# Moving the store of the pairs' decay rows ahead of the second and third weight tiles, in a planned attention-and-two-MLP kernel

## The chip, the cores and the metric

The kernel runs on one core of one Trainium2 chip. The metric is the device time of one execution in microseconds (us), as the median of several runs. A core has TensorE (PE in the profile), VectorE (DVE), ScalarE (ACT), GpSimd (POOL) and SyncE (SP). Nearly every DMA of this kernel is issued from SP's instruction queue and served by 16 DMA engines.

## The reference

Causal attention with a decay per position, then two MLPs with a squared ReLU:

```python
scores = scale * np.matmul(q, k.transpose(0, 1, 3, 2))       # q, k, v: (4, 8, 576, 64)
cum = np.cumsum(np.log(np.clip(f, 0.0001, 1.0)), axis=-1)    # f: (4, 8, 576)
decay = cum[:, :, :, None] - cum[:, :, None, :]
scores = np.where(causal, -1000000000.0, scores + decay)
attn = softmax(scores)
x = (attn @ v) as (2304, 512)
x = np.maximum(x @ moe_w_in, 0.0) ** 2 @ moe_w_out           # 512 -> 2048 -> 512
return np.maximum(x @ moe2_w_in, 0.0) ** 2 @ moe2_w_out
```

## The kernel before

Nothing is written in program order by hand. Each piece of work is an `op(engine, duration, function, priority, dependencies, buffers)`. The planner `Plan.run` (line 106) plays all of them through with the given durations and picks, whenever an engine is free, the ready op with the lowest priority number; the order in which it picks is the order in which the instructions are emitted. Ops that may run on either of two engines (`either`, line 324) get the one that is free in that play. So a change in one op's priority or dependencies can reorder every engine from there on.

The work has these stages.

- **Head.** SP loads `f`, the first 64 positions of q and k (`load_qk`, L469) and the first weight tile in two halves (L798). DVE and ACT make the log and the running sum of `f` (L1335 to L1349). L472 stores the first 64 positions' decay rows beside q and k. `first_part` (line 458) does the attention of the first 64 positions, for two halves of the heads: scores L486, softmax L492 to L502, transposes L514, product with v L526, and the split of the result into a high and a low part (L541, L543), which is the input of the first MLP block.
- **Pairs.** `pair` (line 555) does positions 64 to 191, for two heads at a time, 16 times. q and k come by L567, the decay rows by L570 from the buffer `aug2_d` in DRAM, v by L573. The scores are L589, the maximum L409 on DVE, the exponential L417, the normalisation L605 (ACT) or L607 (DVE or POOL), the transposes L615, their copy L618, the product L628/L629, the copy to X L636.
- **Weights.** Meanwhile the 16 tiles of the first MLP (`weights`, line 783) are loaded in an integer form (L798, 1024 KB each) into three staging buffers (`st`, `ph`, `tmp`), decoded on DVE by L816, L818 and L820 (the last tile by L823 to L829), and split into a high part on ACT (L833) and a low part on DVE (L837).
- **First MLP and the remaining attention.** Blocks of 12 matmuls (L861 into `hp`, L936 into `yp`) fill PE between the attention's pieces; between the two, `hidden` squares the ReLU (L870, then L873 on DVE, L880 on ACT or L877 on POOL) and splits it (L883, L886). `unit` (line 643) does positions 192 to 575 of each head (L713, L731, L750).
- **Second MLP.** L1233 and L1259, from about 600 us to the end.

PE also has filler matmuls (L1384) that the planner puts where PE would stand idle in the head.

The op that is changed is `store2` (line 1362, the DMA is L1363): one DMA of 96 KB from X to `aug2_d`, which all 16 pairs read through L570. Its values are written by `times8_act` (L1360, on ACT). Before the change it depends on those and on `first_loads` (the four L472 stores), with priority -1.0e7. The second half of the first weight tile has priority U + 3 and the v loads of the head U + 4 and U + 5, where U is -1.0e9; a lower number goes first.

Of the kernel before, what the change touches and what calls it, by code (L numbers as in the profile page):

```python
# [69 lines left out]
class Plan:  # L70
# [17 lines left out]
    def op(self, eng, dur, fn, prio, deps=(), uses=(), data=None, other=None, dmas=1, rows=128):  # L88


        o = Op()
        o.how, o.uses, o.data, o.dmas, o.rows, o.turn = {eng: (dur, fn, 0)}, tuple(uses), data, dmas, rows, dur == self.TURN[0]
        if other:
            o.how[other[0]] = (other[1], other[2], 1)
        o.prio = (prio, len(self.ops))
        o.outs, o.ready, o.nwait = [], 0.0, 0
        for d in deps:
            if d is not None:
                d.outs.append(o)
                o.nwait += 1  # L100
        for b in o.uses:
            b.left += 1
        self.ops.append(o)
        return o
# [122 lines left out]
def act(n, psum=False):  # L227
    return (0.052 if psum else 0.093) + 0.00083 * n
# [34 lines left out]
def attention_then_two_squared_relu_mlps(  # L263
# [26 lines left out]
    P = Plan()  # L290
    op = P.op
# [69 lines left out]
    U = -1.0e9  # L361
# [921 lines left out]
    with tc.manual_schedule():  # L1283
# [81 lines left out]
        def parts(y):  # L1365
            if y == 0:
                nc.scalar.mul(out=ch, in_=f_cum, mul=8.0)
            elif y == 1:
                nc.vector.scalar_tensor_tensor(out=cl, in0=f_cum, scalar=8.0, in1=f32(ch), op0=ALU.mult, op1=ALU.subtract)
            else:  # L1370
                nc.scalar.mul(out=nh, in_=f32(ch), mul=-1.0)
                nc.scalar.mul(out=nl, in_=f32(cl), mul=-1.0)
# [25 lines left out]
        first_done, first_loads = [], []  # L1398
# [1 line left out]
            first_part(y, -1.0e8 + y)  # L1400
        o = op("DVE", 0.67, scan1, -1.0e7, [o_f])
        o_8 = op("ACT", 2 * act(QA), times8_act, -1.0e7, [o, o_m1])
        aug_second = [op("SP", P.COPY[0], store2, -1.0e7, [o_8] + first_loads, data=0.3)]
        o_p = op("ACT", act(S), lambda: parts(0), TUNE["PP"], [o] + first_done)
        o_p = op("DVE", dvs(S), lambda: parts(1), TUNE["PP"], [o_p])
        o_p = op("ACT", 2 * act(S), lambda: parts(2), TUNE["PP"], [o_p])
# [118 lines left out]
```

## Time and profile before

| what | before |
|---|---|
| median of 3 runs | 972.8 us (972.77 to 976.41) |
| profiled execution, own time | 977.94 us |
| its span, first to last instruction | 976.2 us |
| PE busy | 948.3 us (97%) |
| DVE / ACT / POOL busy | 683.6 / 453.1 / 361.4 us |
| mean granted PE clock | 0.982 of full speed |

Full speed of the clock is 2.4 GHz, and 0.50 is the lower level, 1.2 GHz. Busy times are sums over an engine's instructions; "idle before" is the time for which an engine stood still just ahead of an instruction, with what released it. Where a stretch lists "PE 62.0 of 68.0", the rest is idle.

### The profile page before, as it was taken

How to read it: one execution, taken by the hardware profiler on the slowest of the kernel's cores; microseconds unless marked ns; L12 is line 12 of the kernel's file. 1: busy time of each engine (PE TensorE's matmuls, PEld its weight loads, DVE VectorE, ACT ScalarE, POOL GpSimd, SP SyncE). 2: the span in 40 equal slices, each digit the busy share in tenths (PEclk: the TensorE clock that was granted, in tenths of full speed). 3: DMA queues.
4: the chain of work that ended last, by engine and by line, in shares of the span. 5: the costliest groups of instructions: out<-in, count | busy, mean ns of one | idle time of the engine just before them, and what ended most of it. 6: DMA issues, size and time to landing. Idle time of an engine off the chain costs nothing.

```text
span 976.2 us, 17134 instructions
## 1 busy us (share of the span) xinstructions
PE 948.3 (97%) x6463; PEld 866.7 (89%) x6463; DVE 683.6 (70%) x1341; ACT 453.1 (46%) x900; POOL 361.4 (37%) x315
## 2 busy tenths in 40 slices
PE   6999999999999999999999999999999999999997
PEld 3888898999997999999999998988898988989886
DVE  7998667787768778876478689888874445734343
ACT  3686677777777678775333353223230112311011
POOL 2244443444434435434232435332351314522130
PEclk7799999999999999999999999999999999999999
DMA  8767245666656756755546524674452111322113
GB/s 251 253 202 207 83 104 119 140 129 146 132 110 134 148 122 134 143 118 120 120 160 207 173 82 157 199 242 159 134 171 88 64 65 65 117 86 79 65 65 108
DMA packets 177187, 131.91 MB, mean 135 GB/s; under 512 B 140944, under 2 KB 155536, under 8 KB 175056
## 3 DMA queue, kind: packets, MB, share of 16 engines
q1 hardware_dynamic: 176848, 130.32, 49.1%
q8 instruction: 51, 0.84, 0.4%
q10 hardware_dynamic: 256, 0.49, 0.2%
q14 instruction: 32, 0.26, 0.1%
HBM read 85.07 MB, written 18.42 MB: 106 GB/s over the span
## 4 chain that ended last, share of the span: by engine, by line
PE 70%; DVE 11%; issue 9%; POOL 3%; ACT 3%; DMA 2%; POOLq 0%; SPq 0%; ACTq 0%; DVEq 0%
PE yp L936 16%; PE hp L861 16%; PE hp L1233 13%; PE bk L1259 10%; PE bk L750 5%; PE yp L1259 5%; PE bk L713 4%; POOL g L1246 2%; DVE ph L439 1%; DVE tmp L818 1%; DVE tmp L820 1%; DVE pp L409 1%; DVE w L1122 1%; POOL gt L886 1%; DVE w L837 1%
## 5 line engine op out<-in xcount | busy, mean ns | idle before, releaser
L936 PE MATMUL yp<-gt,w 128*128 128x256 f32 x1728 | 231.6, 283 | 1.8 <-POOL gt L886 1.7
L861 PE MATMUL hp<-xk,w 128*128 128x256 f32 x1728 | 227.7, 282 | 1.1 <-DVE w L837 0.8
L936 PEld LDWEIGHTS yp<-gt,w 128*128 128x128 f32 x1728 | 216.5, 189 | 6.2 <-POOL gt L886 3.1
L861 PEld LDWEIGHTS hp<-xk,w 128*128 128x128 f32 x1728 | 215.3, 190 | 3.0 <-DVE w L837 1.0
L886 POOL TENSOR_TENSOR gt<-sq,gt 128x512 fp32r<-128x512 f32 x72 | 97.3, 1352 | 154.4 <-ACT gt L883 135.9
L1259 PE MATMUL bk<-w,g 128*128 128x512 f32 x576 | 148.5, 394 | 0.7 <-POOL g L1246 0.7
L1246 POOL TENSOR_TENSOR g<-r,g 128x768 fp32r<-128x768 f32 x36 | 66.8, 1855 | 203.2 <-ACT g L1245 199.3
L1233 PE MATMUL hp<-w 128*128 128x384 f32 x630 | 123.9, 335 | 0.1
L1259 PEld LDWEIGHTS bk<-w,g 128*128 128x128 f32 x576 | 106.6, 188 | 18.7 <-POOL g L1246 1.6
L1245 ACT CAST g<-r 128x768 fp32r<-128x768 f32 x47 | 39.3, 835 | 180.1 <-DVE r L1244 180.0
L1233 PEld LDWEIGHTS hp<-w 128*128 128x128 f32 x630 | 111.7, 188 | 8.1 <-DVE st L1210 0.4
L417 ACT ACTIVATE pp<-pp,stat 128x448 f32<-128x448 f32 (+1 forms) x128 | 78.4, 613 | 44.6 <-DVE stat L409 37.0
L439 DVE SCALAR_TENSOR_TENSOR ph<-pp,stat,ph 128x320 f16<-128x320 f32 (+2 forms) x96 | 77.3, 814 | 15.5 <-ACT ph L432 13.9
L1210 DVE TENSOR_TENSOR r<-hp,st 128x384 f32<-128x384 f32 x62 | 34.5, 556 | 62.8 <-PE hp L1233 62.7
L448 POOL TENSOR_TENSOR vv<-vv 128x320 f32<-128x320 f32 x64 | 54.4, 850 | 54.8 <-DMA vv<-in_v_dram 42.1
L1244 DVE SCALAR_TENSOR_TENSOR r<-r 128x768 f32<-128x768 f32 x47 | 73.6, 1567 | 1.4
L1259 PE MATMUL yp<-w,g 128*128 128x512 f32 x288 | 74.5, 393 | 0.0
L1233 PE MATMUL hp<-w,far 128*128 128x384 f32 x378 | 74.1, 335 | 0.0
L870 ACT ACTIVATE sq<-hp 128x512 f32<-128x512 f32 x72 | 42.8, 594 | 66.8 <-PE hp L861 66.3
L1233 PEld LDWEIGHTS hp<-w,far 128*128 128x128 f32 x378 | 67.3, 188 | 4.7
L409 DVE CUSTOM_DVE_ANT_0 pp<-bk,mask 128x448 f32<-128x448 f32 (+1 forms) x128 | 59.4, 476 | 15.3 <-PE bk L713 9.9
L873 DVE SCALAR_TENSOR_TENSOR sq<-hp,sq 128x512 f32<-128x512 f32 x64 | 44.0, 688 | 35.1 <-ACT sq L870 34.7
(171 smaller groups left out, 1281.5 us busy)
## 6 DMA issues: line engine op xcount, KB each, us to landing
w<-wo_d SPq DMA_DIRECT2D x48, 512.0 KB
stage<-in_w_dram SPq DMA_DIRECT2D x26, 512.0 KB
raw<-in_qk_dram SPq DMA_DIRECT2D x32, 288.0 KB
wo_d<-part SPq DMA_DIRECT2D x16, 512.0 KB
ph<-in_w_dram SPq DMA_DIRECT2D x7, 1024.0 KB
st<-in_w_dram SPq DMA_DIRECT2D x6, 1024.0 KB
vv<-in_v_dram SPq DMA_DIRECT2D x32, 160.0 KB
qk_a<-in_qk_dram SPq DMA_DIRECT2D x16, 192.0 KB
```

Of the source, the lines that this page charges most:

```text
L409: nc.vector.tensor_tensor_reduce(out=x[:rows, c0:c0 + wd], in0=src, in1=msk, scale=-0.125, scalar=3.0e38 if first else nmax[:rows, 5:6], o ...
L417: nc.scalar.activation(out=x, in_=x, func=AF.Exp, scale=-1.0, bias=nmax[:rows, t:t + 1], accum_out=ssum[:rows, t:t + 1])
L439: nc.vector.scalar_tensor_tensor(out=flat[:rows, z:z + wd], in0=x, scalar=r, in1=flat[:rows, 128 * blk:128 * blk + wd], op0=ALU.mult, op1= ...
L448: eng.tensor_tensor(out=vv()[:, :, 1] if i == 0 else x.bitcast(BF16)[:, :, 0::2], in0=x, in1=x.bitcast(BF16)[:, :, 1::2], op=ALU.subtract)
L750: nc.tensor.matmul(dst.rearrange("p (n c) -> p n c", n=rh.shape[1]), lhsT=lt, rhs=rh, start=(i == 0), stop=(i == len(todo) - 1), skip_grou ...
L861: nc.tensor.matmul(ps, lhsT=lt, rhs=rh, start=(k_ == 0 and c == 0), stop=(k_ == KD - 1 and c == 2))
L886: eng.tensor_tensor(out=gt[1]()[:, :c], in0=sq()[:, :c], in1=f32(gt[0]()[:, :c]), op=ALU.subtract)
L936: nc.tensor.matmul(yp[d // 2]()[:, d % 2], lhsT=lt, rhs=rh, start=(i == 0 and c == 0 and d % 2 == 0), stop=(i == NF - 1 and c == 2), skip_ ...
L1233: nc.tensor.matmul(ps()[:, 0:TH], lhsT=lt, rhs=rh, start=(k_ == 0 and c == 0), stop=(k_ == 1 and c == 2))
L1244: o = op("DVE", dvs(TU), lambda r=r: nc.vector.scalar_tensor_tensor(out=r(), in0=r(), scalar=0.0, in1=r(), op0=ALU.max, op1=ALU.mult), e0, ...
L1246: l = either_vp(TU, lambda e, r=r, g=g: e.tensor_tensor(out=g()[:, 1], in0=r(), in1=f32(g()[:, 0]), op=ALU.subtract), e0, [h], [r, g])
L1259: nc.tensor.matmul(bank(ob[c]), lhsT=g()[:, a, c * 128:(c + 1) * 128], rhs=rw()[:, b], start=(p == 0 and x == 0 and z == 0), stop=(p == NP ...
```

## The change

```diff
-        aug_second = [op("SP", P.COPY[0], store2, -1.0e7, [o_8] + first_loads, data=0.3)]
+        aug_second = [op("SP", P.COPY[0], store2, U + 2.5, [o_8], data=0.3)]
```

The store no longer depends on the L472 stores, and its priority puts it ahead of the weight tile's second half (U + 3) and of everything else that is then waiting on SP. No operation is added or removed; the planner makes a new order for all engines.

On SP, in the head: `st`, `ph` and `tmp` from `in_w_dram` are the first, second and third weight tiles' loads, `aug_d<-X` is the store.

```order
 L469 DMA tmp<-in_qk_dram 64x2048
 L472 DMA tmp<-tmp 1x16x128 x4
+L1363 DMA aug_d<-X 32x2x384
 L798 DMA st<-in_w_dram 128x1024
 L476 DMA tmp<-in_v_dram 128x512 x2
 L798 DMA ph<-in_w_dram 128x2048
 L798 DMA tmp<-in_w_dram 128x2048
-L1363 DMA aug_d<-X 32x2x384
```

The store has moved up past five DMAs; the nine that follow it (three L567, L798, L573, L570, L573 and two L570) keep their order.

On DVE, at the end of the head: L409 with `bk_87` is the first pair's maximum, L543 is the low part of the first MLP block's input.

```order
 L820 SCALAR_TENSOR_TENSOR tmp<-tmp 128x1024
 L818 SCALAR_TENSOR_TENSOR tmp<-st,tmp 128x1024
+L409 ISA pp_106,stat<-bk_87,mask_111 128x192
+L409 ISA stat 128x1
 L543 TENSOR_TENSOR xk_83<-bk_90,xk_83 128x2x64
 L543 TENSOR_TENSOR xk_84<-bk_90,xk_84 128x2x64
```

One half of the first pair's maximum now stands ahead of the four L543.

On DVE, at the end of the pairs, where the last weight tile is made (L823 to L829 decode it, the L837 from `ph` is its low part). Before:

```order
L825 SCALAR_TENSOR_TENSOR ph<-ph 128x1024
L837 TENSOR_TENSOR w<-tmp,w 128x2x512
L423 TENSOR_SCALAR stat<-stat 128x2
L426 RECIPROCAL stat<-stat 128x2
L827 TENSOR_SCALAR ph<-ph 128x1024
L829 TENSOR_TENSOR ph<-ph 128x1024
L837 TENSOR_TENSOR w<-ph,w 128x2x512
```

And with the change:

```order
L827 TENSOR_SCALAR ph<-ph 128x1024
L426 RECIPROCAL stat<-stat 128x2
L409 ISA pp_107,stat<-bk_88,mask_111 128x192
L409 ISA stat 128x1
L636 COPY X<-bk_90 128x128
L829 TENSOR_TENSOR ph<-ph 128x1024
L423 TENSOR_SCALAR stat<-stat 128x2
L426 RECIPROCAL stat<-stat 128x2
L607 TENSOR_SCALAR pp_107<-pp_107,stat 128x192 x2
L837 TENSOR_TENSOR w<-ph,w 128x2x512
```

The last pair's maximum, reciprocal and normalisation (L607) now stand ahead of the last tile's low part. Over the whole stage up to that L837 the new order has ten more instructions on DVE: seven L607, which were L605 on ACT, one L618 and two L636 that were on ACT. Two squares (L877) have gone from POOL to ACT (L880).

## Rows read from the trace of the kernel before

**Rows 1.** Busy time of each engine, from the page

```profile
PE 948.3 (97%) x6463; PEld 866.7 (89%) x6463; DVE 683.6 (70%) x1341; ACT 453.1 (46%) x900; POOL 361.4 (37%) x315
```

**Rows 2.** Stretches of the span: us, busy times, then PE clock, DMA share, GB/s

```profile
13.44:31.82 18.38, 13.77 (x126) 9.04 (x124) 18.34 (x31) 6.70 (x15) 3.55 (x4) 0.59 0.91 295
...
44.99:113.46 68.47, 63.19 (x494) 59.64 (x492) 61.68 (x126) 51.22 (x140) 31.98 (x41) 0.98 0.64 193
113.46:480.00 366.54, 362.05 (x2909) 333.50 (x2908) 266.18 (x721) 259.24 (x532) 155.99 (x154) 1.00 0.60 125
...
970.70:976.20 5.50, 0.24 (x2) 0.00 (x0) 0.69 (x1) 0.23 (x1) 0.00 (x0) 0.97 0.69 218
```

**Rows 3.** Timeline of SP's DMA issues in the head: start, duration, instruction

```profile
8.74 0.58 SPq L798 DMA_DIRECT2D st<-in_w_dram  x1
...
11.79 0.35 SPq L1363 DMA_DIRECT2D aug_d<-X  x1
...
17.94 0.57 SPq L573 DMA_DIRECT2D vv<-in_v_dram  x1
21.55 0.30 SPq L570 DMA_DIRECT2D qk_a<-aug_d  x1
```

**Rows 4.** What SP's queue waited for: us in total, times, longest

```profile
SPq L570 <- DMA aug_d<-X: 3.0, 1, 3.0
```

**Rows 5.** DMA rates in two stretches of the head, and sizes of issues there

```profile
12.50:19.00 6.50, 5.63 (x55) 3.22 (x51) 5.52 (x12) 1.67 (x2) 0.00 (x0) 0.50 0.91 358
19.00:26.00 7.00, 3.94 (x43) 2.48 (x43) 7.00 (x12) 2.32 (x4) 0.00 (x0) 0.68 1.06 287
...
st<-in_w_dram SPq DMA_DIRECT2D x1, 1024.0 KB
qk_a<-in_qk_dram SPq DMA_DIRECT2D x3, 192.0 KB
```

**Rows 6.** Timeline of PE where the head ends; idle before in brackets

```profile
26.86 1.81 PE L589 MATMUL bk<-qk_a 66*128 66x192 f32 x6 [0.68 <-DMA qk_a<-aug_d]
28.61 0.37 PE L526 MATMUL bk<-tmp 64*64 64x64 f32 x2
...
32.78 2.72 PE L861 MATMUL hp<-xk,w 128*128 128x256 f32 x11 [0.18 <-DVE xk L543]
```

**Rows 7.** Timeline of DVE at the same place

```profile
32.05 0.47 DVE L543 TENSOR_TENSOR xk<-bk,xk 128x128 fp32r<-128x128 f32 x2
...
33.98 0.34 DVE L409 CUSTOM_DVE_ANT_0 pp<-bk,mask 128x192 f32<-128x192 f32 x1
```

**Rows 8.** Timelines of DVE and PE where the last weight tile is ready

```profile
111.80 1.29 DVE L837 TENSOR_TENSOR w<-ph,w 128x1024 fp32r<-128x1024 f32 x1 [1.25 <-ACT w L833]
...
113.46 1.57 PE L861 MATMUL hp<-xk,w 128*128 128x256 f32 x12
114.87 1.57 PE L936 MATMUL yp<-gt,w 128*128 128x256 f32 x12
```

**Rows 9.** Timelines of DVE and POOL: prices of the operations that change engines

```profile
14.05 0.42 DVE L816 TENSOR_SCALAR tmp<-st 128x512 uint32<-128x512 uint32 x1
...
36.22 0.15 DVE L423 TENSOR_SCALAR stat<-stat 128x2 f32<-128x2 f32 x1
...
49.71 0.28 DVE L636 COPY X<-bk 128x128 f32<-128x128 f32 x1
...
65.23 1.00 DVE L423 TENSOR_SCALAR stat<-stat 128x2 f32<-128x2 f32 x1
...
64.69 1.51 POOL L877 TENSOR_TENSOR sq<-sq 128x512 f32<-128x512 f32 x1 [1.07 <-ACT sq L870]
```

**Rows 10.** Two short stretches in the pairs' stage, columns as in Rows 2

```profile
70.00:73.00 3.00, 2.06 (x18) 1.86 (x17) 3.00 (x6) 1.85 (x5) 2.27 (x4) 1.00 0.61 86
...
75.00:78.00 3.00, 3.00 (x16) 3.00 (x15) 3.00 (x7) 1.51 (x5) 0.00 (x0) 0.50 0.94 251
```

**Rows 11.** What DVE waited for between 44.99 and 113.46 us

```profile
DVE tmp L816 <- DMA st<-in_w_dram: 2.6, 1, 2.6
```

## Prediction

> **What bounds the kernel now.** I read the busy times first. PE works 948.3 of 976.2 us [rows 1], so only 28 us of the span are not PE work, and a change that adds or removes no matmul can win no more than a part of those, and of the time that PE spends at its lower clock. The stretches say where they lie [rows 2]: 18.38 - 13.77 = 4.6 us in the second part of the head, 68.47 - 63.19 = 5.3 us in the pairs' stage, 366.54 - 362.05 = 4.5 us in the stage of the units, 5.3 us after the last matmuls; the rest lies elsewhere. The same rows show the second bound: DVE is busy 18.34 of 18.38 us in the head and 61.68 of 68.47 us in the pairs' stage. So up to 31.8 us the time is set by DVE's queue, and from there by PE with DVE close behind.
>
> Next I read SP's timeline and its waits, to see what the moved store holds up. It is issued at 11.79 us [rows 3]. The first load that reads what it wrote is L570; the L573 just ahead of it on SP is out at 17.94 + 0.57 = 18.51 us, and L570 goes out at 21.55 us, after a wait of 3.0 us for the store to land [rows 3, 4]. That wait is what the change aims at. Last I read PE and DVE where the first scores of a pair (L589) and the first MLP block begin [rows 6, 7], and where the last weight tile is ready [rows 8].
>
> **The change, part by part.**
>
> *The store goes out earlier.* It would start where the weight tile's second half starts now, at 8.74 us, 3.05 us earlier [rows 3]. Everything that it passes is issued one store issue later, 0.35 to 0.4 us. The only one of those with a reader soon after is the second half of the first weight tile, issued over 8.74 to 9.32 us and decoded by L816 at 14.05 us [rows 3, 9]. Half a tile is 512 KB, or 0.52 MB; at 287 to 358 GB/s [rows 5] that is 1.5 to 1.8 us, so some 2.9 us of the 4.7 us between are left for what stands ahead of it and for landing. I cost the delay at 0; without that cover it would be 0.4 us.
>
> *SP's wait of 3.0 us.* It goes: L570 can be issued at about 18.5 us. I do not expect the rows to land 3 us earlier. When L570 is issued, three loads of 192 KB and one of 1024 KB stand ahead of it in both versions [rows 3, 5], together 1,600 KB or 1.64 MB, which take 4.6 us at 358 GB/s and 5.7 us at 287 GB/s; the DMA engines are 0.91 and 1.06 busy there, so they have nothing to catch up with. The change orders the same bytes differently; the load stays behind all of them. And the reader gains little if the load does come early: L589 waited for it only 0.68 us [rows 6], and the new order puts a filler matmul of some 0.4 us in front. Behind L589 stand L526 and the split of the first MLP block's input, and that is done on DVE by L543 at 32.05 us, in a queue that has no gap from 13.4 us on [rows 2, 7]. Late next is therefore DVE's queue, as before. I take 0; bounds: 0 and a gain of 0.7 us.
>
> *L409 ahead of L543.* One L409 of 0.34 us now runs before the four L543 [rows 7], and the first MLP block already waited for L543, 0.18 us at 32.78 us [rows 6]. Nothing covers this: **+0.3 us**. Bounds 0 and 0.4 us (with its read-out row).
>
> *Ten more instructions on DVE up to the last weight tile.* The trace before has no L607. Its nearest rows are a TENSOR_SCALAR of 512 columns, 0.42 us, and one of 2 columns, 0.15 us [rows 9]; at 192 columns the line between them gives 0.25 us, so seven are 1.75 us. Two L636 are 0.56 us [rows 9]. An L618 of 384 columns lies between one L636 and three of them, 0.28 to 0.84 us; I take the middle, 0.55 us. Together 2.9 us. Against that, two squares leave POOL. While such a square ran (64.69 us, 1.51 us) a DVE instruction that takes 0.15 us elsewhere took 1.00 us [rows 9], so each may give DVE back 0.85 us, 1.7 us for two. Net +1.2 us, with bounds 0 and +2.9 us. What of it reaches PE? The last tile's low part ends at 111.80 + 1.29 = 113.09 us, and PE takes the block that needs it at 113.46 us; it then still has a block that needs no new tile (L936 at 114.87 us) [rows 8], which is 1.41 us of cover. +1.2 us stays under it: **0 us**; bounds 0 and 1.5 us. The last pair's softmax that now stands ahead of that L837 lies beside ACT's work for the same tile, for which DVE waited 1.25 us anyway [rows 8].
>
> *All else* is the same work in another order, with the pieces of the pairs spread more evenly on PE: the old order has three places with four or more attention pieces in a row, the new one has one. I give that no term, but it bounds the range.
>
> Sum: +0.3 us. On the profiled execution that is 977.94 to 978.3 us. The profiled execution is 5.1 us above the median of the runs shown (972.8 us), so for the median I say 972.8 + 0.3 = **973.1 us**.
>
> **Rivals.**
>
> *Slower: the weight tiles set the pace of the pairs' stage.* The place is PE's wait for the last tiles. If the squares give nothing back, DVE has 2.9 us more. One tile that came late cost DVE 2.6 us [rows 11], since on SP a tile's load stands behind a v load that waits for PE; the new order makes other such neighbours. Two more of these make 5.2 us. From 1.4 us of delay on, PE pays: 2.9 + 5.2 - 1.4 + 0.3 = +7.0 us, **979.8 us**. For it: DVE is 90% busy there [rows 2]. Against: the net is small and POOL's squares do show in DVE's rows.
>
> *Faster: the new order takes away waits.* Half of PE's 5.3 and 4.5 us of idle time [rows 2] is 4.9 us, and the stretch at the lower clock at 75 us [rows 10], worth 3.00 x 0.5 = 1.5 us, need not come again: -6.4 + 0.3 = -6.1 us, **966.7 us**. For it: the even spread. Against: the planner uses fixed durations in both versions, and nothing in the rows ties these waits to the store.
>
> *The clock falls elsewhere.* Before, PE was busy 2.06 of 3.00 us around 71 us at full clock, and then worked at 0.50, 1.2 GHz, through 75 to 78 us [rows 10]. One fall more or less is 1.5 us: **974.6** or 971.6 us. The Trainium skill says in "TensorE: Matmul & The Clock Gate", section "HAM oscillation — how this bites in real kernels", that a PE which pauses between bursts is throttled again and starts the next burst slow, each time anew. By that rule the fall follows the pauses and moves with the order; the trace agrees here, in one place.
>
> *The store pays in full.* If DVE did not hold the head, the 3.0 us of SP's wait would come off: 972.8 - 3.0 + 0.3 = **970.1 us**. Against: DVE's 18.34 of 18.38 us. The Trainium skill, "DMA: Bandwidth & Descriptors", section "Queues, rings and completion order", says that each of the 16 rings takes its descriptors in order, but that a small transfer on few rings may complete ahead of a wide one issued earlier. By that the two-row load could pass the weight tile; no run here shows it yet.
>
> **Numbers.** 0.5% (4.9 us) is about what a measurement of this kernel can tell from no change. Chances: the forecast 0.48, a moved clock fall 0.20, the store in full 0.05 (these three within 0.5%: 0.73), faster 0.11, slower 0.16. The range of 967 to 980 us reaches to both outer rivals and leaves out about half of each.
>
> **What would show it.** Right: L1363 at about 8.7 us, no wait of L570 for `aug_d<-X`, L589 still at 26 to 27 us, the first full MLP block at about 33.1 us, the last tile's L837 ending by 114.5 us, PE busy near 948 us. Wrong: a first MLP block before 32 us (the store paid), the last L837 after 119 us (the tiles set the pace), or PE idle in the pairs' and units' stages together below 5 us or above 15 us.

## The result, and the profile after

The changed kernel takes **982.0 us** (median of 6 runs, 980.35 to 984.08) where the kernel before took 973.9 us beside it (6 runs, 972.47 to 976.41): ratio 1.0083, 95% interval 1.0063 to 1.0103. It is 8.2 us slower; I had said 973.1 us, and the range of 967 to 980 us does not hold the result. The profiled execution took 982.51 us. The one of before took 977.94 us and so lay above its own median; its trace and the one after are only 4.6 us apart, and the control run below gives a trace of before that is nearer to its median.

The store does what the change says. SP's timeline in the head after the change:

```profile
8.43 0.49 SPq L1363 DMA_DIRECT2D aug_d<-X  x1
8.96 0.42 SPq L798 DMA_DIRECT2D st<-in_w_dram  x1
...
18.45 0.58 SPq L573 DMA_DIRECT2D vv<-in_v_dram  x1
19.09 0.50 SPq L570 DMA_DIRECT2D qk_a<-aug_d  x1
```

The store goes out 3.4 us earlier than in [rows 3], and L570 follows L573 at once; the wait of [rows 4] is gone. PE at the end of the head, and DVE at the last weight tile:

```profile
27.39 1.70 PE L589 MATMUL bk<-qk_a 66*128 66x192 f32 x6 [0.22 <-issue]
...
33.09 3.27 PE L861 MATMUL hp<-xk,w 128*128 128x256 f32 x12 [0.72 <-ACT xk L541]
```

```profile
110.67 1.23 DVE L837 TENSOR_TENSOR w<-ph,w 128x1024 fp32r<-128x1024 f32 x1 [0.40 <-ACT w L833]
```

The first MLP block begins 0.3 us later than in [rows 6], and the last weight tile is ready 1.2 us earlier than in [rows 8]. PE waits for a tile's low part (L837) once, 0.6 us and for the last tile but one, where it waited 0.8 us before; for the last tile it does not wait. So the tiles do not make the loss, and of the head's delay no more than 0.3 us shows here. The busy times of the page, and the stretches of [rows 2] (us, busy times of PE, PE's weight loads, DVE, ACT and POOL, then PE clock, DMA share, GB/s):

```profile
PE 947.0 (97%) x6461; PEld 867.3 (88%) x6463; DVE 681.9 (70%) x1356; ACT 453.3 (46%) x892; POOL 357.1 (36%) x308
```

```profile
44.99:113.46 68.47, 61.55 (x496) 59.88 (x495) 62.33 (x137) 49.01 (x128) 37.55 (x45) 0.98 0.63 191
113.46:480.00 366.54, 357.89 (x2846) 328.40 (x2845) 259.98 (x720) 259.12 (x530) 153.43 (x145) 0.99 0.59 124
```

PE's busy time is that of the first trace of before within 1.3 us. What has grown against that trace is its idle time: 68.47 - 61.55 = 6.9 us in the pairs' stage (5.3 before) and 366.54 - 357.89 = 8.7 us in the units' stage (4.5 before), 15.6 us together where I had named 15 us as the mark of a wrong prediction. Among PE's waits (total, times, longest) the first two here have grown most against before, where they were 1.7 and 1.2 us in all; the third is the one for a tile:

```profile
PE yp L936 <- POOL gt L886: 4.5, 4, 3.0
PE bk L713 <- DMA qk<-aug_d: 4.0, 3, 2.7
...
PE hp L861 <- DVE w L837: 0.6, 1, 0.6
```

Three places stand out. **The POOL place**, near 65 us, on PE's timeline and then on POOL's and DVE's:

```profile
63.02 0.28 PE L936 MATMUL yp<-gt,w 128*128 128x256 f32 x1
66.34 1.72 PE L936 MATMUL yp<-gt,w 128*128 128x256 f32 x11 [3.04 <-POOL gt L886]
```

```profile
60.11 3.77 POOL L579 COPY vv<-vv 64x64 f32<-64x64 f32 x4 [2.89 <-DMA vv<-in_v_dram]
63.96 2.33 POOL L886 TENSOR_TENSOR gt<-sq,gt 128x512 fp32r<-128x512 f32 x1
...
63.93 1.23 DVE L837 TENSOR_TENSOR w<-tmp,w 128x1024 fp32r<-128x1024 f32 x1 [0.16 <-ACT w L833]
```

The copies of two pairs' v (L579, two copies each) stand ahead of the L886 on which an MLP block waits. POOL first stands 2.89 us for the v load, then copies for 3.77 us. The planner assumes 0.4 us for such a pair of copies; here they took 1.9 us. The L886 itself then takes 2.33 us; it starts 0.03 us behind an L837 on DVE. In the order of before two pairs' copies stand ahead of the same L886 too, each one pair earlier, and PE does not wait for it. This is the same place in the control run described below, on POOL and on PE:

```profile
58.16 2.53 POOL L579 COPY vv<-vv 64x64 f32<-64x64 f32 x4 [7.54 <-DMA vv<-in_v_dram]
60.77 1.29 POOL L886 TENSOR_TENSOR gt<-sq,gt 128x512 fp32r<-128x512 f32 x1
```

```profile
61.38 0.71 PE L628 MATMUL bk<-pt,vv 128*128 128x128 f32 x4
...
63.62 0.71 PE L628 MATMUL bk<-pt,vv 128*128 128x128 f32 x4 [0.26 <-ACT pt L618]
...
64.31 1.66 PE L936 MATMUL yp<-gt,w 128*128 128x256 f32 x12
```

There four attention pieces in a row (L628, L615, L589, L628), 2.9 us from 61.38 us on, stand on PE between the last L861 block and the L936 block, and L886 is done at 62.06 us, before PE asks for it at 64.31 us. In the changed order no attention piece stands between the two blocks.

**The PE place**, near 118 us, where the second group of the first MLP begins. PE's timeline, then its stretches:

```profile
116.21 0.38 PE L861 MATMUL hp<-xk,w 128*128 128x256 f32 x1 [0.55 <-ACT xk L909]
117.37 0.85 PE L861 MATMUL hp<-xk,w 128*128 128x256 f32 x5 [0.78 <-DVE xk L913]
118.06 0.28 PE L936 MATMUL yp<-gt,w 128*128 128x256 f32 x1
119.10 2.72 PE L936 MATMUL yp<-gt,w 128*128 128x256 f32 x11 [0.76 <-POOL gt L886]
```

```profile
116.00:119.00 3.00, 1.35 (x7) 0.95 (x7) 1.73 (x2) 1.29 (x3) 2.27 (x2) 0.97 0.00 0
119.00:122.00 3.00, 2.90 (x13) 2.90 (x14) 0.00 (x0) 0.00 (x0) 0.05 (x1) 0.50 0.00 0
```

Three waits follow each other, PE is busy 1.35 of 3.00 us, and the next 3 us run at 0.50, which is 1.2 GHz: 13 matmuls, where the run with the store alone (below) does 28. Behind the POOL place, too, the clock of this trace stands at 0.50, from 68 to 71 us.

**The L713 place**, near 180 us, in the units:

```profile
176.88 0.54 PE L713 MATMUL bk<-qk 128*128 128x288 f32 x2
177.25 1.58 PE L861 MATMUL hp<-xk,w 128*128 128x256 f32 x12
178.66 0.30 PE L713 MATMUL bk<-qk 128*128 128x320 f32 x1
181.67 0.80 PE L713 MATMUL bk<-qk 68*128 68x320 f32 x3 [2.70 <-DMA qk<-aug_d]
```

One unit's last scores free the buffer for the next unit's operands, and between the two the new order leaves one MLP block, 1.4 us. The load of the next decay rows was issued at 177.45 us and PE stands until 181.67 us.

### The profile page after: what moved, and what is told of

Same layout as the page of the kernel before. It is cut to its first block, busy times and chain, and to the rows that moved or that the text cites. A ratio compares the mean times of both kernels' runs of the same rounds, so it can differ in the third digit from the quotient of the medians.

```text
span 980.7 us, 17119 instructions
## 1 busy us (share of the span) xinstructions
PE 947.0 (97%) x6461; PEld 867.3 (88%) x6463; DVE 681.9 (70%) x1356; ACT 453.3 (46%) x892; POOL 357.1 (36%) x308
## 4 chain that ended last, share of the span: by engine, by line
PE 71%; issue 10%; DVE 9%; POOL 4%; DMA 3%; ACT 2%; POOLq 0%; SPq 0%; ACTq 0%; DVEq 0%
PE yp L936 16%; PE hp L861 16%; PE hp L1233 13%; PE bk L1259 10%; PE bk L750 5%; PE yp L1259 5%; PE bk L713 4%; POOL g L1246 2%; DMA qk<-aug_d 1%; DVE w L1122 1%; POOL gt L886 1%; DVE tmp L818 1%; DVE w L837 1%; DMA st<-in_w_dram 1%; DVE tmp L820 1%
## 5 line engine op out<-in xcount | busy, mean ns | idle before, releaser
L936 PE MATMUL yp<-gt,w 128*128 128x256 f32 x1728 | 231.5, 282 | 4.8 <-POOL gt L886 4.5
L861 PE MATMUL hp<-xk,w 128*128 128x256 f32 x1728 | 229.1, 283 | 2.8 <-DVE xk L913 0.8
L936 PEld LDWEIGHTS yp<-gt,w 128*128 128x128 f32 x1728 | 216.2, 189 | 8.9 <-POOL gt L886 6.0
L861 PEld LDWEIGHTS hp<-xk,w 128*128 128x128 f32 x1728 | 216.0, 190 | 5.5 <-ACT xk L541 1.4
L886 POOL TENSOR_TENSOR gt<-sq,gt 128x512 fp32r<-128x512 f32 x72 | 100.1, 1391 | 162.7 <-ACT gt L883 142.5
L1246 POOL TENSOR_TENSOR g<-r,g 128x768 fp32r<-128x768 f32 x32 | 59.3, 1853 | 215.8 <-ACT g L1245 215.8
L439 DVE SCALAR_TENSOR_TENSOR ph<-pp,stat,ph 128x320 f16<-128x320 f32 (+2 forms) x96 | 74.2, 775 | 16.6 <-ACT ph L432 14.8
L1244 DVE SCALAR_TENSOR_TENSOR r<-r 128x768 f32<-128x768 f32 x47 | 71.5, 1520 | 1.4
L432 ACT ACTIVATE ph<-pp,stat 128x320 f16<-128x320 f32 (+2 forms) x96 | 63.0, 664 | 15.9 <-DVE stat L426 12.0
```

The source lines that it names most:

```text
L432: nc.scalar.activation(out=a, in_=x, func=AF.Copy, scale=r)
L439: nc.vector.scalar_tensor_tensor(out=flat[:rows, z:z + wd], in0=x, scalar=r, in1=flat[:rows, 128 * blk:128 * blk + wd], op0=ALU.mult, op1= ...
L861: nc.tensor.matmul(ps, lhsT=lt, rhs=rh, start=(k_ == 0 and c == 0), stop=(k_ == KD - 1 and c == 2))
L886: eng.tensor_tensor(out=gt[1]()[:, :c], in0=sq()[:, :c], in1=f32(gt[0]()[:, :c]), op=ALU.subtract)
L936: nc.tensor.matmul(yp[d // 2]()[:, d % 2], lhsT=lt, rhs=rh, start=(i == 0 and c == 0 and d % 2 == 0), stop=(i == NF - 1 and c == 2), skip_ ...
L1244: o = op("DVE", dvs(TU), lambda r=r: nc.vector.scalar_tensor_tensor(out=r(), in0=r(), scalar=0.0, in1=r(), op0=ALU.max, op1=ALU.mult), e0, ...
```

## The experiments

Theory A: the planner's new order on all engines makes the loss, and the store is innocent. Rival B: the store's place on SP makes it. To part them, most runs read the order from a written list of (operation, engine, buffers) in place of planning it; the diffs below are then diffs of that list, as instructions of one engine or as its parts.

```diff
     def run(self):
-        import heapq
+        return replay(self)
```

All ratios are to runs of the kernel before taken beside each.

| run | median us | ratio, 95% interval |
|---|---|---|
| order of before from the list | 974.7 | 0.9998 [0.9985, 1.0012] |
| store alone moved | 973.6 | 0.9993 [0.9980, 1.0007] |
| order alone | 983.3 | 1.0084 [1.0066, 1.0101] |
| store moved, no new plan | 974.3 | 0.9995 [0.9983, 1.0007] |
| changed order to the pairs' end, then before's | 976.3 | 1.0010 [0.9998, 1.0022] |
| before's to the pairs' end, then the changed | 981.3 | 1.0067 [1.0050, 1.0085] |
| changed order to 224 us, then before's | 984.1 | 1.0104 [1.0082, 1.0126] |
| changed order to 164 us, then before's | 980.6 | 1.0068 [1.0054, 1.0083] |
| changed order to 197 us, then before's | 983.2 | 1.0080 [1.0060, 1.0100] |
| swap on POOL in the changed order | 979.0 | 1.0046 [1.0028, 1.0064] |
| the same swap, before's order from the pairs' end | 974.5 | 0.9995 [0.9983, 1.0008] |
| swap on PE in the changed order | 981.1 | 1.0060 [1.0043, 1.0077] |
| both swaps in the changed order | 976.9 | 1.0023 [1.0012, 1.0034] |
| both swaps, before's order from 164 us | 976.3 | 1.0012 [1.0000, 1.0023] |
| new plan, transposes 0.38 | 980.7 | 1.0068 [1.0048, 1.0087] |
| new plan, scores 0.85 | 983.1 | 1.0088 [1.0067, 1.0109] |
| new plan, product with v 0.59 | 981.2 | 1.0062 [1.0040, 1.0084] |

### Store or order

**The control** is the list of before, unchanged.

> The order of before, read from a list that was written down from its planner instead of being planned again: the same instructions in the same order on every engine, the store behind the second and third weight tile as before. Every theory expects the time of before, ratio 1.000, about 974 us: it is the control for the runs whose order is a changed list, and gives a second trace of the kernel before, whose first one was taken on an execution 4 us above its median. In that trace PE should idle some 5.3 us in the pairs' stage and 4.5 us in the units' stage again if those figures belong to the order, and other figures if they belong to that one execution.

It took 974.7 us, ratio 0.9998: a list in place of the planner costs nothing. Its stretches:

```profile
44.99:113.46 68.47, 63.08 (x516) 60.36 (x515) 59.55 (x124) 52.37 (x141) 37.62 (x49) 1.00 0.61 183
113.46:480.00 366.54, 361.03 (x2917) 332.68 (x2917) 267.10 (x721) 258.57 (x532) 154.71 (x147) 1.00 0.61 128
```

PE idles 5.4 and 5.5 us here, 10.9 us together (9.8 in the first trace of before), and its clock stays at 1.00 in both stages. So some 5 us more idle time in these two stages go with the new order. Over the whole span the comparison with this trace reads otherwise: PE is busy 940.4 us of 973.2 here and 947.0 us of 980.7 in the changed kernel, so it idles 32.8 and 33.7 us. In the rest of the span the changed kernel idles less (18.1 against 21.9 us), and its busy time is 6.6 us longer, in part because its clock fell (0.98 and 0.99 in the two stages). Idle time in two traces does not place the 8 us, then; the runs below do. The fall of the clock in [rows 10] does not come in this execution, but it belongs to no order: the run with the store alone has one near 88 us instead, and the run that moves the store without a new plan shows it again at the same place:

```profile
75.00:78.00 3.00, 3.00 (x19) 3.00 (x19) 3.00 (x8) 1.84 (x5) 0.15 (x1) 0.62 1.02 285
```

**The store alone**, in the order of before, on SP:

```diff
 L472 DMA tmp<-tmp 1x16x128 x4
+L1363 DMA aug_d<-X 32x2x384
 L798 DMA st<-in_w_dram 128x1024
 L476 DMA tmp<-in_v_dram 128x512 x2
 L798 DMA ph<-in_w_dram 128x2048
 L798 DMA tmp<-in_w_dram 128x2048
-L1363 DMA aug_d<-X 32x2x384
```

> The order of before on every engine, with one thing moved: the store L1363 stands on SP ahead of the second half of the first weight tile, where the change put it. Theory A (the moved store is innocent; the 8.2 us come from the new order that the planner made on all engines): 973 to 975 us, ratio 0.998 to 1.001, SP's wait of 3 us for the store gone, L589 at 26 to 27.5 us. Rival B (the store, by delaying what stands behind it on SP and in the DMA queue, starts a delay that the pairs' stage carries on): 980 to 983 us, the rows of the first weight tile about 0.5 us late. Rival C (both carry a part): 977 to 979 us. My own earlier rival, the store pays in full: 970 to 971 us.

973.6 us, ratio 0.9993: theory A, and no gain to be told from nothing. The time falls where A put it, but L589 comes 0.8 us later than the latest that I gave it. SP, PE and DVE in this run:

```profile
17.07 0.33 SPq L798 DMA_DIRECT2D st<-in_w_dram  x1
...
18.14 0.54 SPq L570 DMA_DIRECT2D qk_a<-aug_d  x1
```

```profile
28.27 1.86 PE L589 MATMUL bk<-qk_a 66*128 66x192 f32 x6 [2.05 <-DMA qk_a<-aug_d]
```

```profile
29.09 0.69 DVE L816 TENSOR_SCALAR tmp<-st 128x1024 uint32<-128x1024 uint32 x1 [0.38 <-DMA st<-in_w_dram]
```

L570 is issued at 18.14 us, where the control issued it at 21.43 us, and the rows still arrive only at some 28.2 us; the control's L589 began at 26.82 us. The weight tile issued 1.07 us ahead of L570 (17.07 us) lets DVE start at 29.09 us, so the small load did end ahead of the large one, by some 0.8 us. That is how the Trainium skill puts it in "DMA: Bandwidth & Descriptors", section "Queues, rings and completion order": completion does not follow the order of issue. Here it is worth little, since both end 10 to 12 us after their issue. Over all traces of this document L589 began at 26.5 to 28.9 us with the early store (twelve traces) and at 26.0 to 27.2 us with the late one (seven). The early issue brings the rows no sooner.

**The order alone**: the changed order with the store back in its old place.

```diff
 L472 DMA tmp<-tmp 1x16x128 x4
-L1363 DMA aug_d<-X 32x2x384
 L798 DMA st<-in_w_dram 128x1024
 L476 DMA tmp<-in_v_dram 128x512 x2
 L798 DMA ph<-in_w_dram 128x2048
 L798 DMA tmp<-in_w_dram 128x2048
+L1363 DMA aug_d<-X 32x2x384
```

> The order of the changed kernel on every engine, but the store L1363 put back behind the third weight tile on SP, where it was before. Theory A (the new order costs the 8.2 us): 981 to 983 us, ratio 1.007 to 1.010, PE idle about 7 us in the pairs' stage and 8 to 9 us in the units' stage, the wait of about 3 us of L936 for L886 near 63 us there again. Rival B (the store's place costs them): 973 to 975 us, ratio 1.000, and the waits gone. Rival C (both): 977 to 979 us.

983.3 us, ratio 1.0084: the whole loss without the store's move, and rival B is out. PE idled 6.8 and 8.2 us in the two stages, and the 3.0 us wait was there again. The stall near 180 us was too, but 1.4 us of it were put down to L674, a copy on DVE, and not to the load. The three waits of the PE place came as well, with PE busy 1.35 of 3.00 us as in the changed kernel, but the clock did not fall behind them:

```profile
118.00:121.00 3.00, 1.35 (x7) 0.96 (x7) 1.73 (x2) 1.50 (x3) 2.27 (x2) 1.00 0.00 0
121.00:124.00 3.00, 2.69 (x22) 2.69 (x23) 0.00 (x0) 0.00 (x0) 0.26 (x1) 1.00 0.00 0
```

So the whole loss does not need that fall.

**The store moved without a new plan.** This is how the change could have been written: the store stands ahead of the second and third tiles, behind the first tile's second half.

```diff
-        aug_second = [op("SP", P.COPY[0], store2, -1.0e7, [o_8] + first_loads, data=0.3)]
+        aug_second = [op("SP", P.COPY[0], store2, -1.0e7 + 3, [o_8], data=0.3)]
```

> The store ahead of the second and third weight tiles by another number: its priority stays with the head's own, three units behind them, instead of the pairs' one. With it the planner keeps the order of before on PE, DVE, ACT and POOL, and only SP's order differs. Theory A (only the new order costs): 973 to 975 us, ratio 0.998 to 1.001, as the list with the store alone moved gave. Rival (there is something to gain from the store, which that run's place ahead of the first tile's second half spoilt): 971 to 972 us.

974.3 us, ratio 0.9995: theory A again. The store's move by itself is worth nothing measurable, in either place.

### Which part of the order

```diff
-order = before
+order = changed, to the last operation of the pairs; then before
```

> The order of the changed kernel (store included) up to the last operation of the pairs, and from there the order of before. By the two traces, the changed order idles PE 1.6 us more in the pairs' stage and 4.1 us more in the units' stage, and has about 0.5 us more in the head; the rest of the 8.2 us is not placed by them. Theory A1 (most of it comes from the order in the units' stage): 975 to 977 us here, ratio 1.001 to 1.003. Theory A2 (most comes from the order in the head and the pairs' stage, the later idle time being its echo): 979 to 983 us, ratio 1.005 to 1.010.

976.3 us, ratio 1.0010: A1. The interval holds 1, so the first half of the order is not told from before's.

```diff
-order = before
+order = before, to the last operation of the pairs; then changed
```

> The order of before up to the last operation of the pairs, the store in its old place, and from there the order of the changed kernel: the counterpart of the run with the two halves the other way round, which took 976.3 us, ratio 1.0010. Theory A1 (the order in the units' stage carries most of the loss, the parts add up): 980 to 982 us, ratio 1.006 to 1.008, with PE's wait for the rows of aug_d near 180 us and the idle time and lower clock near 384 us again, and without the wait for L886 near 65 us. Rival (the units' loss needs the pairs' loss before it, because it shifts the units against the DMA transfers): 974 to 976 us.

981.3 us, ratio 1.0067, and the two halves add up (0.10% + 0.67% against 0.83%). The larger part needs nothing of the pairs' order. In this run too PE pauses where the second group begins, and its clock then falls:

```profile
113.00:116.00 3.00, 1.36 (x7) 0.95 (x7) 1.73 (x2) 1.21 (x3) 2.24 (x2) 1.00 0.00 0
116.00:119.00 3.00, 2.98 (x16) 2.98 (x17) 0.00 (x0) 0.00 (x0) 0.00 (x0) 0.62 0.00 0
```

Next I let the changed order run on into the units, first to 224 us:

```diff
-order = changed
+order = changed, to 224 us; then before
```

> The order of the changed kernel (store included) up to an operation that runs at some 222 us, and from there the order of before. The changed kernel's own order loses time near 118 us, near 180 us and near 385 us; the order of before loses about as much near 305 us as the other does near 385 us. Theory (the net loss lies between 115 and 220 us, the later places cancel): 980 to 983 us, ratio 1.006 to 1.009. Rival (it lies in the later part of the units): 975 to 977 us, like the run that left the changed order at the end of the pairs, 976.3 us.

984.1 us, ratio 1.0104: the rival is out, though the time lies just above what I gave the theory. I took the L713 place for the cause, since it has the longest wait, and put the change of order on either side of it:

```diff
-order = changed
+order = changed, to 164 us; then before
```

> The order of the changed kernel (store included) up to the product with v that runs at 162.5 to 164.4 us, and from there the order of before: the waits near 118 us stay, and between two units' scores PE has four MLP blocks again, not one, so the stall of 2.7 us near 180 us should not come. Theory (that stall and what follows it up to 200 us carry the units' part of the loss, some 4 to 5 us): 977 to 979.5 us, ratio 1.002 to 1.005. Rival (it lies in what comes before 164 us or after 197 us): 981 us or more.

```diff
-order = changed
+order = changed, to 197 us; then before
```

> As the run before it, but the changed order kept up to the MLP block at 195.6 to 197 us, so that it takes in the one-block place near 178 us. Theory: the stall comes, and the time is that of the run that kept the changed order up to 224 us, 982 to 985 us, ratio 1.007 to 1.011. Rival: the same time as the run that changes over at 164 us, within 1.5 us.

980.6 and 983.2 us, ratios 1.0068 and 1.0080. The first lies between the theory (979.5 us at most) and the rival (981 us or more), the second in its theory's range. **My theory of the L713 place fell:** the stall was to carry 4 to 5 us, and the two differ by 2.6 us in their medians and by 0.12%, 1.2 us, in their ratios. In the first of the two the stall did not come, as PE's timeline shows, with four MLP blocks between one unit's scores and the next:

```profile
177.16 0.81 PE L713 MATMUL bk<-qk 128*128 128x288 f32 x4
177.80 1.58 PE L936 MATMUL yp<-gt,w 128*128 128x256 f32 x12
...
182.05 1.57 PE L861 MATMUL hp<-xk,w 128*128 128x256 f32 x12
183.46 0.86 PE L713 MATMUL bk<-qk 128*128 128x320 f32 x4
```

It was still 6.7 us slower than before. What the stall is worth the two intervals do not tell from nothing. The traces say only that it costs idle time: between 165 and 200 us PE idles 2.3 to 3.3 us wherever the changed order stands there, and 0.3 us at most where the order of before does. Between the pairs' end (1.0010) and 164 us (1.0068) lies the PE place.

### Which place

**The swap on POOL**, in the changed order:

```diff
 L579 COPY vv_104<-vv_104 64x64 x2
-L579 COPY vv_103<-vv_103 64x64 x2
-L886 TENSOR_TENSOR gt_80<-sq_77,gt_79 128x512
+L886 TENSOR_TENSOR gt_80<-sq_77,gt_79 128x512
+L579 COPY vv_103<-vv_103 64x64 x2
 L886 TENSOR_TENSOR gt_82<-sq_78,gt_81 128x512
```

> The order of the changed kernel, with one swap on POOL alone: the L886 for which PE waits 3.0 us near 65 us runs ahead of the second of the two pairs of L579 copies before it. The first pair of copies ends at about 62.0 us, so L886 can end near 64 us instead of 66 us and the wait of PE shrinks from 3.0 to about 1.1 us. Theory (PE's idle time there is lost for good): 980 us, 1.9 us less than the changed kernel's 982 us, ratio 1.006. Rival (the pairs' stage is paced by the weight tiles, so that PE waits later for what it did earlier): 981.5 to 982.5 us, ratio 1.008, the last L629 as late as before the swap.

979.0 us, ratio 1.0046. POOL's timeline, and the wait that is left on PE:

```profile
60.79 1.58 POOL L579 COPY vv<-vv 64x64 f32<-64x64 f32 x2 [7.32 <-DMA vv<-in_v_dram]
62.45 1.26 POOL L886 TENSOR_TENSOR gt<-sq,gt 128x512 fp32r<-128x512 f32 x1
63.67 1.44 POOL L579 COPY vv<-vv 64x64 f32<-64x64 f32 x2
```

```profile
63.77 2.71 PE L936 MATMUL yp<-gt,w 128*128 128x256 f32 x11 [1.31 <-POOL gt L886]
```

The wait went from 3.04 to 1.31 us, the L886 from 2.33 to 1.26 us, and the median by 3.0 us: the theory, and rather more than it said. (This trace is of the slowest of its executions, 982.89 us; it shows the place and not the time.)

```diff
-order = changed, to the last operation of the pairs; then before
+order = changed with the swap on POOL, to the last operation of the pairs; then before
```

> The run that has the changed order up to the end of the pairs and the order of before behind it (976.3 us), with the swap on POOL near 62 us added, which alone took the changed kernel from 982 to 979 us. Theory (the wait near 65 us is lost for good and is what the pairs' part of the loss consists of): 973 to 974.5 us, ratio 0.998 to 1.000. Rival (the swap's gain in the other run came from elsewhere): 976 us.

974.5 us, ratio 0.9995: the theory's time, and with this one swap the changed head and pairs are as fast as before's. But the interval overlaps that of the run without the swap (1.0010), so the gain of 1.8 us is not shown by these two alone.

**The swap on PE** moves one block of L936 behind the L861 block that follows it, as it stands in the order of before:

```diff
 L861 MATMUL hp_91<-xk_85,w 128x256 x6
 L861 MATMUL hp_91<-xk_83,w 128x256 x6
-L936 MATMUL yp_93<-gt_81,w 128x256
-L936 MATMUL yp_93<-gt_82,w 128x256
...
 L861 MATMUL hp_91<-xk_85,w 128x256 x6
 L861 MATMUL hp_91<-xk_83,w 128x256 x6
+L936 MATMUL yp_93<-gt_81,w 128x256
+L936 MATMUL yp_93<-gt_82,w 128x256
...
```

> The order of the changed kernel with one swap on PE near 118 us: the second L861 block of the next group runs ahead of the L936 block that waits 0.76 us for its L886 there, as in the order of before (two L861 blocks, then the L936). Then that L936 starts 1.4 us later and finds its input ready. Theory (that wait, and the clock that falls to 0.50 behind it for 3 us, are lost for good, 0.8 + 1.5 us): 979.5 to 980.5 us, ratio 1.005 to 1.006, granted clock 1.00 from 119 to 122 us. Rival (the clock falls all the same, because the two waits for xk before it stay): 981.5 to 982.5 us, ratio 1.008.

```diff
-order = changed
+order = changed, with the swap on POOL and the swap on PE
```

> Both swaps in the order of the changed kernel: the one on POOL near 62 us, which alone gave 979.0 us, and the one on PE near 118 us. Theory (the losses add up): 976.5 to 977.5 us, ratio 1.002 to 1.004; what is left over before, some 2 to 3 us, is the stall near 180 us. Rival (each gain is taken back by a later wait): 979 to 980 us.

981.1 us, ratio 1.0060, with the swap on PE alone (its median lies between theory and rival, its ratio agrees with the theory), and 976.9 us, ratio 1.0023, with both, as the theory said. The stretches of the run with both:

```profile
113.00:116.00 3.00, 1.74 (x13) 1.34 (x11) 1.12 (x2) 2.12 (x4) 1.04 (x1) 1.00 0.00 0
116.00:119.00 3.00, 2.93 (x24) 2.93 (x25) 0.61 (x2) 0.68 (x2) 1.57 (x1) 1.00 0.00 0
119.00:122.00 3.00, 3.00 (x28) 3.00 (x27) 1.38 (x2) 1.24 (x3) 1.30 (x1) 1.00 0.00 0
```

The two waits for xk stay, the third is gone, and the clock does not fall. The run with the swap on PE alone shows the same 1.00 from 113 to 125 us. In the traces of this document all three waits stand at this place nine times, and the clock fell behind them five times; the two waits for xk alone stand there five times, and it fell behind none. That points to the third wait and does not prove it.

So two swaps of neighbours take the ratio from 1.0083 to 1.0023, some 6 of the 8 us, and the intervals lie apart. One at a time: with the swap on PE in both runs, the swap on POOL takes 1.0060 to 1.0023, intervals apart; with the swap on POOL in both, the swap on PE takes 1.0046 to 1.0023, and these intervals overlap a little. So the gain of the swap on POOL is shown by itself, that of the swap on PE is likely.

The trace of the run with the swap on PE alone is of its fastest execution, 977.49 us against a median of 981.1 us. In it PE waited only 0.76 us at the POOL place, with POOL's order unchanged, and the L886 took 1.27 us. So the order makes the place, but not every execution pays for it in full.

```diff
-order = changed, to 164 us; then before
+order = changed with both swaps, to 164 us; then before
```

> The changed order up to 164 us and the order of before behind it, which took 980.6 us without any stall near 180 us, with both swaps in its first part. Theory (its loss over before, 6.7 us, is made of the wait near 65 us and the wait and clock near 118 us, and not of anything later): 975 to 976.5 us, ratio 1.000 to 1.002. Rival (there is a further loss behind 164 us at the change of order): 978 us or more.

976.3 us, ratio 1.0012: the theory. Of the 0.68% of the same run without the swaps, 0.56% are gone, so the change-over at 164 us and what follows it cost nothing large. Against the run with both swaps and the changed order to the end (1.0023) it leaves 0.11%, 1.1 us, for the L713 place and all else behind 164 us; the intervals overlap.

### Is it this plan, or any other

Three kernels have the store in its old place and one assumed duration of the planner changed by 5 or 10 ns, in turn:

```diff
-        o_tr = op("PE", 0.375, tr, prio, p_ops, [pp, o])
+        o_tr = op("PE", 0.38, tr, prio, p_ops, [pp, o])
```

> The kernel before with the store in its old place, and one number of the planner changed by 5 ns: the duration that it assumes for a pair's transposes (0.375 becomes 0.38). No instruction is added, removed or changed, but the planner answers with another order on all engines, about as different from before as the changed kernel's. Theory A (what I missed is that any new plan redraws the waits of pairs and units): a time that is off 974.5 us by something like the 8 us of the change, on either side, 966 to 985 us. Rival (plans are all alike in time, and the changed kernel's loss is due to what the store's new time tells the planner): 973 to 976 us.

```diff
-        o_s = op("PE", 0.84, sc, prio, [ld, o_aug], [x, bk], rows=66)
+        o_s = op("PE", 0.85, sc, prio, [ld, o_aug], [x, bk], rows=66)
```

> As the run before it, with another number: the duration that the planner assumes for a pair's scores, 0.85 instead of 0.84. Again another order on all engines and the store in its old place. Theory A: off 974.5 us by several us on either side, and not by the same amount as the run before it. Rival (plans are all alike): 973 to 976 us.

```diff
-        o_av = op("PE", 0.6, av, prio + TUNE["pq"], [o_tr, ov], [pT, vv, o])
+        o_av = op("PE", 0.59, av, prio + TUNE["pq"], [o_tr, ov], [pT, vv, o])
```

> A third new plan from the kernel before with the store in its old place: the duration that the planner assumes for a pair's product with v becomes 0.59 instead of 0.60. The two before it took 980.7 and 983.1 us. Theory (the order of before is an unusually good one, and any other plan is some 6 to 9 us slower, the change's own among them): 979 to 984 us. Rival (plans scatter to both sides, two slower ones were chance): below 975 us is as likely as above.

980.7, 983.1 and 981.2 us, ratios 1.0068, 1.0088 and 1.0062. All three are slower, by as much as the change. I had expected scatter to both sides in the first two, and that did not come. The waits of PE in the second and in the first of them:

```profile
PE yp L936 <- POOL gt L886: 4.6, 5, 3.0
```

```profile
PE yp L936 <- POOL gt L886: 1.4, 3, 0.8
```

The POOL place is in the one and not in the other, and the intervals of their ratios overlap. They share the L713 place (PE is busy 6.33 to 6.37 of the 8 us from 176 to 184 us in all three) and pauses between 113 and 125 us (busy 9.89, 9.89 and 10.50 of 12 us, the last at a clock of 0.86), in the first two the three waits of the PE place. What the loss of these three is made of I did not take apart.

One rival stands untested. The kernel's priorities (`TUNE`, line 30) hold numbers like AP1=201.48 and pq=-119.59. They look as if they had been chosen by trying many plans and keeping a fast one; if so, nearly any new plan would be slower, for no reason in the change. The record does not say how they were chosen.

## Why the prediction was wrong

- **The store's move, its delay of the first tile, SP's wait** (0, 0 and 0 us): right. The store alone gives 0.9993 and 0.9995. The reason was right too: L570 went out 3.3 us earlier in the run with the store alone and its rows came no sooner. The rival that the store pays in full is out.
- **L409 ahead of L543** (+0.3 us): the first MLP block did begin 0.3 us later (33.09 against 32.78 us), but that agreement is luck. PE waited there for L541 on ACT, 0.72 us, and not for L543 on DVE, and in that execution the head was 0.5 us late already at L589 (27.39 against 26.86 us). The two traces of before (32.78 and, in the control, 31.82 us) lie further apart than the term; with the order alone the block began at 32.31 us. No run shows the term by itself.
- **Ten more instructions on DVE** (0 us, under a cover of 1.41 us): right in what reached PE. The last L837 ended at 110.67 + 1.23 = 111.90 us (108.96 us in the control), where I had set 113.09 + 1.4 us as the point from which PE would pay, and PE did not wait for it. The rival in which the weight tiles set the pace, my only slower one, named a time near the outcome (979.8 us) for a reason that is not in the trace: luck.
- **"All else is the same work in another order ... I give that no term, but it bounds the range."** This is the step that failed. I read the new order as an even spread of the pairs' pieces on PE, saw fewer runs of attention pieces in it, and priced what it could do only as a gain (the rival that the new order takes away waits, 966.7 us). But a run of attention pieces is also work that covers a wait: one of the three places with four or more pieces in a row is the one that stands ahead of the L936 block in the control's timeline above. With the change PE comes to that block without them, while POOL comes later to its L886, and the wait is open. (This is read from the two timelines; no run put the pieces back.) The new order brought three waits of 3.0, 0.8 and 2.7 us, and in its trace the clock fell behind the first two. The order alone costs the whole loss (1.0084). Two pairs of neighbours in it, on POOL near 62 us and on PE near 118 us, carry 0.60%, 5.8 us; the L713 place and the rest account for the other 0.23%.
- **The clock** (one fall, 1.5 us): I priced it alone, as a rival; in the changed kernel's trace it came on top of two waits. Behind 119 us PE did 13 matmuls in 3 us and not 28. Nor does it move with the order alone, as I had assumed: it comes and goes between executions of one order. The Trainium skill says in "TensorE: Matmul & The Clock Gate", section "HAM oscillation — how this bites in real kernels", that a PE which pauses is throttled again and starts the next burst slow; the trace agrees near 119 us, and the run with the order alone, busy 1.35 of 3.00 us from 118 us and at 1.00 behind it, shows that not every such pause does it.

Nearly all my signs of being right came true (the store at 8.43 us, no wait of L570, the first block at 33.09 us, the last L837 by 114.5 us, PE busy 947 us; only L589 was late): they watched places where nothing happened. The order could have shown the POOL place. With the change the L936 block stands right behind the L861 blocks, with no attention piece between, and the trace of before has the durations of POOL's copies and the waits for the v loads; I looked at the places where DVE's queue had changed, since DVE was the second bound, and at no place where POOL's or PE's had.

What stays open: how much the L713 place costs; why the swap on POOL is worth some 1.8 us ahead of before's order and 3 to 4 us ahead of the changed one; and why the order of before beats four other plans of the same planner. The places do not add up to the halves, either: without any POOL place, the order of before up to the pairs' end and the changed one behind it still lost 0.67%, and the swap on PE was not run there. No version ran measurably faster than before.

## What to carry to other kernels

Where a planner orders the work from assumed durations, a change of one priority is two changes: the move that was meant, and a new order of everything behind it. Price the second from the order itself, engine by engine, at the places where a waiting instruction has new neighbours ahead of it or has lost those that covered its wait, and try the first without the second, by a priority or a list that leaves the other engines' order alone; here that took one number. Before blaming or praising a change that brings a new plan, run two or three plans that differ by nothing of substance: here they alone cost 0.6 to 0.9%.

## What was not expected of the hardware

- In the run with the store alone a 6 KB load issued at 18.14 us ended at some 28.2 us, and in the control the same load, issued 3.3 us later, ended at 26.8 us. What holds such a load lies behind its issue; what it is, these runs do not show.
- The two 64 x 64 copies of one L579 took 1.2 to 1.9 us on POOL at the POOL place, about as long as or longer than an L886 of 128 x 512 (1.26 to 1.29 us), by a profile in which POOL's times are rough.
- Where POOL and DVE worked on large tiles at once, the one that started second took longer. The L886 on POOL that started 0.03 us behind an L837 on DVE took 2.33 us, and so it did in every trace in which the POOL place cost 3.0 us; in the other traces the same L886 took 1.26 to 1.29 us. In the control the L886 came first, at 60.77 us, and took 1.29 us; the L820 on DVE that started 0.10 us behind it took 2.27 us, against 1.20 us for one at 61.61 us in the changed kernel. Why, these runs do not show. The L820 of the control:

```profile
60.87 2.27 DVE L820 SCALAR_TENSOR_TENSOR tmp<-st,tmp 128x1024 uint32<-128x1024 uint32 x1
```
